# Moving four of six early weight loads behind two units' inputs, and one weight conversion behind a small product

## The chip, the core and the metric

The kernel runs on one core of a Trainium2 chip. The time is the device time of one execution in microseconds (us); less is better. Times of a run with the profiler on are given with their source. In the profile PE is the matrix engine (TensorE), PEld its weight loads, DVE VectorE, ACT ScalarE, POOL GpSimd, and SPq the queue of SyncE, which issues every DMA of this kernel.

## What is computed

Two blocks, one after the other, on float32 data:

```
# attention: batch 4, 8 heads, sequence 768, head size 48
f = 1 / (1 + exp(-f_logit))
for t in range(768):                       # per batch and head
    state = f[t][:, None] * state + outer(k[t], v[t])      # 48 x 48
    y[t]  = q[t] @ state
# mixer: x is y laid out as (4, 768, 384)
h  = (x^T @ U @ V)^T                        # U: 768 x 32, V: 32 x 768
u  = x + h
out = u + max(u @ w_ch1, 0) @ w_ch2         # w_ch1: 384 x 1536, w_ch2: 1536 x 384
```

The four mixer weights come in as 64-bit floats, all other inputs as 32-bit floats.

## The kernel before, in words

**Attention units.** The work of attention is cut into 16 units: a unit is one batch and two heads. A unit's inputs f, k, q and v are each loaded in two or three DMAs (`load`, L376; issued in L387 and L394, from unit 6 on also in L400). Rows of 48 floats make packets of 192 bytes, and a unit is 9 DMAs of 1,152 KB in all. f, k and q have two buffers each, v has three, so the loads of unit n wait until unit n-2 (for v: n-3) has been read. In the first stretch a unit runs through: transposes on PE (`pt`, L506), sigmoid on ACT (L527), two scans on DVE (L540, L558), products on DVE (L518), scores (`sc`, L589), the transposed keys (`kept`, L610), the states (`ds`, L626, scanned on DVE in L647), the output from the states (`y`, L664), then the output within chunks (`y`, L682), and a copy on ACT into the batch's `x` (L688). Ahead of the last matmuls of `y` stands a tiny copy on ACT (`seen`, L671).

**Mixer.** When the four units of a batch are done, its mixer starts: `low_rank` (`ph`, L146, copied by ACT in L149), `added_up` (`ph`, L154, copied by ACT in L156), `mix` (`pu`, L171, added to x by DVE in L161), `turn` (transposes `put`, L181, copied by ACT into `uT` in L182, for three pairs of row blocks), then the first large product `ch1` (`pz`, L193; relu on ACT in L200) and the second (L215 or L238). The mixer of a batch is woven into the attention of the next batch.

**Weights.** `weights` is a list of 27 tiles in this order: U, V in two pieces, 12 tiles of w_ch1 (called w1_0 to w1_11 here; 384 KB each as 64-bit words), 12 tiles of w_ch2. Each tile has a `start`, which issues its DMA (L55), and an `end`, which turns 64-bit floats into 32-bit floats: two instructions on ACT (L64, L65), three on DVE (L66 to L68), one on POOL (L69). U and V land in `w_raw` buffers, of which there are four. w1_0 to w1_5 ("staged": `FIRST = 6`) land in the three `zw` tiles, two in each, which the mixer needs only later. `ahead_by(n, loads)` (L76) starts the first n tiles at once and returns one call for each tile: call i starts tile i+n and then converts tile i.

**What sets the order.** PE, DVE and ACT run in the order in which the program is written (L748, L749). The DMAs stand in SyncE's queue in program order too, and the queue blocks on a DMA whose buffer is not free. In the loop over the first four units (L761 to L776) the order in the queue is: after unit 1's pieces, the v of unit 3 and then `ahead_by(early + FIRST, weights)`, so U, V, V and w1_0 to w1_5; after unit 2's pieces unit 4's f, k, q and v; after unit 3's pieces unit 5's. Behind the loop, L777 and L778 weave the conversions into the end of unit 3: U and the first V ahead of its last matmuls of `y`, and the second V, w1_0 and w1_1 behind its copy into `x`. These five calls also issue the loads of w1_6 to w1_10. Then the loop at L787 runs the mixer's pieces; from its third piece on (`i > 1`) each is followed by one more conversion. Piece 0 is `low_rank`, 1 `added_up`, 2 `mix`, 3 and 4 the first two `turn`, 5 the first `ch1`.

**Filler.** `busy(n)` (L754) issues matmuls on PE whose result nobody reads (`idle`, L756); the kernel has them at places where PE would stand still.

The last part of the kernel, `general_path`, runs only if the inputs are out of the range of the first path; with these inputs it does not run.

Of the kernel before, what the change touches and what calls it, by code (L numbers as in the profile page):

```python
# [20 lines left out]
RAW = 4  # L21
# [53 lines left out]

def ahead_by(n, loads):  # L76

    for start, _ in loads[:n]:
        start()

    def call(i):
        if i + n < len(loads):
            loads[i + n][0]()
        loads[i][1]()

    return [lambda i=i: call(i) for i in range(len(loads))]
# [237 lines left out]
def factored_path(ctx, tc, q, k, v, f_logit, moe_U, moe_V, moe_w_ch1, moe_w_ch2, out, ok):  # L324
# [11 lines left out]
    HP = H // 2  # L336
# [39 lines left out]
    def load(n, *names):  # L376

        b, hp = divmod(n, HP)
        for nm in names:
            if nm == "v":  # L380
                v_tiles[n] = three.tile([P, NBL, 2, D], F32, name="v_nat")
            for par in range(2):
                head = src[nm][b, 2 * hp + par]
                if nm == "v" and par:

                    for s in range(2):
                        nc.sync.dma_start(  # L387
                            out=v_tiles[n][(1 - s) * C : (2 - s) * C, :, par, :],
                            in_=head.rearrange("(c s p) d -> s p c d", s=2, p=C)[s],
                        )  # L390
                    continue
                if nm == "v" or n < TURNED:
                    dst = v_tiles[n] if nm == "v" else nat[n % 2][nm]
                    nc.sync.dma_start(out=dst[:, :, par, 0:D], in_=head.rearrange("(c p) d -> p c d", p=P))  # L394
                    continue
                head = head.rearrange("(c i) d -> i c d", i=NB)
                for part in range(2):
                    p0 = par * PAD + part * NB
                    n_ch = min(NB, D - part * NB)
                    nc.sync.dma_start(  # L400
                        out=raw[n % 2][nm][p0 : p0 + NB, :].rearrange("p (c d) -> p c d", d=NB)[:, :, 0:n_ch],
                        in_=head[:, :, part * NB : part * NB + n_ch],
                    )
# [51 lines left out]
    weights = [take_in(U, moe_U.rearrange("(c p) r -> p c r", p=P))]  # L455
    weights += [take_in(*pair) for pair in by_rows(V, moe_V, R)]
    early = len(weights)
# [10 lines left out]
    FIRST = 6  # L468
# [99 lines left out]
    def mixer(b):  # L568
        return Mixer(tc, b, x_tiles[b], U, V, w1, w2, sums if b else None, ident, blocks, out, two, three, zp, ps_big, ps_mm, b == 0)
# [128 lines left out]
    def front(n, *names):  # L698

        if n >= NU:  # L700
            return []
        if n not in ahead:
            ahead[n] = dict(zip(("gates", "keep", "keys", "read_back", "queries"), prepare(n)))
        return [ahead[n].pop(nm) for nm in names]

    def rear(n, *names):

        if not 0 <= n < NU:
            return []
        if n not in here:  # L710
            here[n] = dict(zip(("kept", "states", "scan", "scores", "read", "inner"), attend(n)))
        return [here[n].pop(nm) for nm in names if nm in here[n]]

    def steps(first, last):


        for n in range(first, last):
            yield from rear(n - 1, "scores") + rear(n, "kept") + front(n + 1, "gates", "keep", "keys")
            yield from rear(n - 1, "read")
            made = rear(n, "states", "scan")  # L720
            yield lambda: [f() for f in made]
            yield from front(n + 1, "read_back", "queries") + rear(n - 1, "inner")
            if n + 2 < NU:
                load(n + 2, "v")

    def attention(pieces, portions, todo):

        fill = Fill(todo, portions)
        for piece in pieces:
            fill()  # L730
            piece()
        fill.rest()

    def start_mixer(b, after):

        m = mixer(b)
        n = len(after) // 4
        pieces = after[:n] + m.before[:1] + after[n : 2 * n] + m.before[1:2] + after[2 * n : 3 * n]
        pieces += m.before[2:3] + after[3 * n :] + m.before[3:]
        for _, piece in pieces:  # L740
            piece()
        return m

    loads = weights

    ctx.enter_context(tc.manual_schedule(engines={nc.tensor.engine}))  # L748
    with tc.manual_schedule(engines={nc.vector.engine, nc.scalar.engine}):  # L749


        idle = ps_mm.tile([P, 512], F32, name="idle", tag="mm")

        def busy(n):  # L754
            for _ in range(n):
                nc.tensor.matmul(idle[:, 0:DM], lhsT=ident, rhs=ends[:, 0:DM], start=True, stop=True)  # L756

        busy(1)
        for piece in front(0, "gates"):
            piece()  # L760
        for n in range(HP):  # L761
            pieces = front(n, "keep", "keys") + rear(n - 1, "scan", "scores")
            pieces += [lambda: busy(3)] + rear(n, "kept") + front(n, "read_back", "queries")
            if n + 1 < HP:
                pieces += front(n + 1, "gates") + rear(n - 1, "read", "inner") + rear(n, "states")
            else:
                pieces += rear(n, "states") + rear(n - 1, "read") + rear(n, "scan", "scores") + rear(n - 1, "inner")
            for piece in pieces:
                piece()
            if n < 2:  # L770
                load(n + 2, "v")
            if n == 1:

                loads = ahead_by(early + FIRST, weights)
            elif n > 1:
                load(n + 2, "f", "k", "q", "v")  # L776
        for piece in rear(HP - 1, "read") + loads[:2] + rear(HP - 1, "inner") + loads[2 : early + 2]:  # L777
            piece()  # L778
        loads = loads[early + 2 :]

        m = mixer(0)
        start = m.before[:5] + m.firsts[0:1] + m.before[5:]
        idles = {1: 1, 2: 1}

        EARLY = 9
        second = chain(front(HP, "gates", "keep", "keys", "read_back", "queries"), steps(HP, 2 * HP + 1))
        for i, (_, piece) in enumerate(start + m.firsts[1:]):  # L787
            busy(idles.get(i, 0))
            piece()
            if loads and i > 1:  # L790
                loads.pop(0)()
            if i >= EARLY:
                next(second)()
        for f in loads:
            f()
        n = len(m.seconds) // (NBL // 2)
        todo, after = m.seconds[:-n], m.seconds[-n:]

        attention(second, 12 + 10 * HP - (len(start) + len(m.firsts) - 1 - EARLY), todo)
        m = start_mixer(1, after)  # L800
        for f in to_sum:
            f()
# [17 lines left out]
def general_path(ctx, tc, q, k, v, f_logit, moe_U, moe_V, moe_w_ch1, moe_w_ch2, out):  # L820
# [16 lines left out]
    HP = H // 2  # L837
# [70 lines left out]
    def load_unit(n):  # L908
        b, hp = divmod(n, HP)
        for nm in "fkq":  # L910
            for par in range(2):
                nc.sync.dma_start(
                    out=nat[n % NSLOT][nm][:, :, par, 0:D],
                    in_=src[nm][b, 2 * hp + par].rearrange("(c p) d -> p c d", p=C),
                )
        v_tiles[n] = three.tile([P, NCH, 2, D], F32, name="v_nat")
        for par in range(2):
            nc.sync.dma_start(
                out=v_tiles[n][:, :, par, :],
                in_=src["v"][b, 2 * hp + par].rearrange("(c p) d -> p c d", p=C),  # L920
            )

    load_weight = weight_loader(nc, two, nc.sync)
    weights = [load_weight(U, moe_U.rearrange("(c p) r -> p c r", p=P))]
# [148 lines left out]
    def mixer(b):  # L1073
        return Mixer(tc, b, x_tiles[b], U, V, w1, w2, None, ident, blocks, out, two, three, zp, ps_big, ps_mm)

    FILLS = NL + 3
    for n in range(NSLOT):
        load_unit(n)
    todo = [(1, f) for f in ahead_by(RAW - 1, weights)]
    for b in range(B):  # L1080
        fill = Fill(todo, HP * FILLS)
        for hp in range(HP):
            attention(b * HP + hp, fill)
        fill.rest()
        m = mixer(b)
        todo = m.before + m.main + m.after
# [59 lines left out]
```

## Time and profile before

| | |
|---|---|
| median of 5 runs | 502.48 us (499.28, 502.42, 502.48, 502.81, 504.44) |
| the profiled execution's own time | 502.67 us |
| its span from first to last instruction | 500.9 us (1.8 us lie around it) |
| PE busy, share of the span | 482.1 us, 96% |
| DVE busy, share | 279.3 us, 56% |
| ACT busy, share | 158.0 us, 32% |
| POOL busy, share | 36.4 us, 7% |
| DMA moved | 34.30 MB, of it 28.70 MB read |
| mean granted clock of TensorE | 0.987 |

The profile's page has the busy share of each engine in 40 slices of 12.5 us; a digit is tenths, 9 means 90% or more. The row PEclk is the TensorE clock that was granted, in tenths of full speed, and the row DMA the mean busy share of the 16 DMA engines. The chain of work that ended last goes back from the last instruction, at each step to what released it; "issue" in it is time for which the profile shows nothing that was waited for. The queue named "instruction" carries the fetches of the engines' own instructions.

### The profile page before, as it was taken

The numbers are of one execution on the slowest core, as the hardware profiler recorded it, in microseconds if no ns is written. First come the engines' busy times: TensorE is split into PE (matmuls) and PEld (weight loads), VectorE is DVE, ScalarE is ACT, GpSimd is POOL, SyncE is SP. The second block draws the span as 40 slices with busy tenths as digits, with TensorE's granted clock in tenths as the row PEclk, the third lists the DMA queues.
The fourth block names the chain that finished last, engine by engine and source line by source line (L and its number), as shares of the span: only waits on it lengthen the run. The fifth ranks groups of instructions, "written<-read, shape, count | busy, mean of one in ns | idle before, by whom it ended". The sixth has DMA issues, their size and how long they took to land.

```text
span 500.9 us, 11989 instructions
## 1 busy us (share of the span) xinstructions
PE 482.1 (96%) x5279; PEld 401.5 (80%) x5279; DVE 279.3 (56%) x402; ACT 158.0 (32%) x297; POOL 36.4 (7%) x49
## 2 busy tenths in 40 slices
PE   6896899999999999999999999999999999999995
PEld 4676588886666568898898788898899888999995
DVE  5884799788998667666764536632411431222232
ACT  3432675654444223324323222413311122101010
POOL 3000355442000000000000000000000000000000
PEclk9997899999999999999999999999999999999998
DMA  9989947675777423325434100100000000000001
GB/s 146 156 182 213 213 122 168 154 152 70 110 111 112 90 41 41 56 26 100 53 48 81 24 33 1 26 1 33 3 1 33 0 35 0 1 31 1 31 2 37
DMA packets 158676, 34.30 MB, mean 68 GB/s; under 512 B 149206, under 2 KB 157078, under 8 KB 158614
## 3 DMA queue, kind: packets, MB, share of 16 engines
q1 hardware_dynamic: 158614, 33.44, 36.4%
q8 instruction: 43, 0.70, 0.6%
q14 instruction: 19, 0.16, 0.1%
HBM read 28.70 MB, written 4.72 MB: 67 GB/s over the span
## 4 chain that ended last, share of the span: by engine, by line
PE 92%; DMA 2%; SPq 2%; DVE 1%; issue 1%; ACT 1%; DVEq 0%; ACTq 0%
PE pz L193 38%; PE pw L238 24%; PE po L215 10%; PE y L664 3%; PE y L682 3%; PE sc L589 3%; PE ds L626 2%; PE pt L506 2%; PE put L181 2%; PE pt L610 1%; SPq L394 1%; PE idle L756 1%; PE ph L146 1%; PE pu L171 1%; DMA f_raw<-in_f_logit_dram 1%
## 5 line engine op out<-in xcount | busy, mean ns | idle before, releaser
L193 PE MATMUL pz<-uT,w 128*128 128x256 f32 x864 | 196.0, 382 | 0.1
L193 PEld LDWEIGHTS pz<-uT,w 128*128 128x128 f32 x864 | 161.0, 190 | 22.4 <-issue 0.3
L200 ACT ACTIVATE z<-pz 128x512 f32<-128x512 f32 x63 | 37.6, 596 | 129.9 <-PE pz L193 125.8
L238 PE MATMUL pw<-w,z 128*128 128x192 f32 x324 | 56.5, 329 | 0.4 <-DVE o L161 0.4
L238 PE MATMUL pw<-zw,w_raw 128*128 128x192 f32 x324 | 55.9, 327 | 0.8 <-DVE o L161 0.8
L238 PEld LDWEIGHTS pw<-zw,w_raw 128*128 128x128 f32 x324 | 53.0, 190 | 2.2 <-DVE o L161 2.1
L238 PEld LDWEIGHTS pw<-w,z 128*128 128x128 f32 x324 | 52.8, 190 | 2.3 <-DVE o L161 1.6
L161 DVE TENSOR_TENSOR w_raw<-z 128x768 f32<-128x768 f32 x18 | 17.2, 955 | 56.3 <-ACT z L200 56.3
L540 DVE TENSOR_TENSOR_SCAN X<-fz,ends 128x768 f32<-128x768 f32 x16 | 28.1, 1757 | 10.3 <-ACT fz L535 5.1
L69 POOL TENSOR_TENSOR w<-w_y,w_r 128x384 int32<-128x384 int32 x24 | 30.2, 1259 | 36.0 <-DVE w_y L68 29.0
L558 DVE TENSOR_TENSOR_SCAN Y<-fz,starts 128x768 f32<-128x768 f32 x16 | 27.9, 1747 | 0.2
L596 DVE TENSOR_TENSOR A<-sc,causal 128x768 f32<-128x768 f32 x16 | 15.2, 949 | 20.4 <-PE sc L589 20.4
L215 PE MATMUL po<-w,zw 128*128 128x384 f32 x72 | 25.6, 499 | 0.0
L215 PE MATMUL po<-w,z 128*128 128x384 f32 x72 | 25.3, 496 | 0.0
L161 DVE TENSOR_TENSOR w_y<-x,pw 128x192 f32<-128x192 f32 x9 | 3.2, 354 | 38.2 <-ACT w_y L251 38.2
L652 ACT COPY st<-added 128x576 f32<-128x576 f32 x12 | 14.7, 1222 | 23.7 <-DVE added L647 23.7
L161 DVE TENSOR_TENSOR w_y<-w_y,pw 128x192 f32<-128x192 f32 x18 | 6.3, 349 | 25.5 <-PE pw L238 25.5
L215 PEld LDWEIGHTS po<-w,zw 128*128 128x128 f32 x72 | 12.9, 189 | 8.7 <-issue 1.2
L215 PEld LDWEIGHTS po<-w,z 128*128 128x128 f32 x72 | 13.1, 190 | 8.5 <-DVE o L161 0.6
L589 PE MATMUL sc<-qT,kz 48*64 48x64 f32 x768 | 15.9, 226 | 4.0 <-issue 4.0
L589 PEld LDWEIGHTS sc<-qT,kz 48*64 48x64 f32 x768 | 13.6, 138 | 7.7 <-issue 7.7
L238 PE MATMUL pw<-w,w_raw 128*128 128x192 f32 x108 | 19.2, 328 | 0.0
(101 smaller groups left out, 527.5 us busy)
## 6 DMA issues: line engine op xcount, KB each, us to landing
w_raw<-in_moe_w_ch_dram SPq DMA_DIRECT2D x18, 384.0 KB, 3.8
out_dram<-o SPq DMA_DIRECT2D x24, 192.0 KB, 2.0
v_nat<-in_v_dram SPq DMA_DIRECT2D x16, 144.0 KB, 3.0
v_nat<-in_v_dram SPq DMA_DIRECT2D x32, 72.0 KB, 2.8
zw<-in_moe_w_ch_dram SPq DMA_DIRECT2D x6, 384.0 KB, 6.1
f_raw<-in_f_logit_dram SPq DMA_DIRECT2D x20, 96.0 KB, 3.1
k_raw<-in_k_dram SPq DMA_DIRECT2D x20, 96.0 KB, 2.8
q_raw<-in_q_dram SPq DMA_DIRECT2D x20, 96.0 KB, 2.9
```

What stands on the lines that cost most here:

```text
L69: nc.gpsimd.tensor_tensor(dst.bitcast(I32), shaped(y.bitcast(I32)), shaped(r), ALU.add)
L161: nc.vector.tensor_tensor(*args)
L193: nc.tensor.matmul(pm[:, i * 2 * P : (i + 1) * 2 * P], lhsT=w1[:, m, o : o + P], rhs=uT[a][:, m, :], start=(m == 0), stop=(m == NDC - 1))
L200: nc.scalar.activation(z[a, c][:, k : k + 2, :].rearrange("p i t -> p (i t)"), pm, AF.Relu)
L215: nc.tensor.matmul(pm, lhsT=z[a, i // NI][:, i % NI, s * P : (s + 1) * P], rhs=w2[:, i, :], start=(i == 0), stop=(i == NFC - 1))
L238: nc.tensor.matmul(pm[:, n * HM : (n + 1) * HM], lhsT=lhs[:, i, :], rhs=rhs[:, i, :], start=(i == 0), stop=(i == NI - 1))
L540: nc.vector.tensor_tensor_scan(backwards(X, S - 1, S), backwards(f, S, S), backwards(ends, S - 1, S), 0.0, ALU.mult, ALU.add,)
L558: nc.vector.tensor_tensor_scan(Y, f[:, 0:S], starts, 0.0, ALU.mult, ALU.add)
L589: nc.tensor.matmul(sc[part[s ^ par], par, c * C : (c + 1) * C], lhsT=T["k"][rows[par], chunk[2 * c + s]], rhs=T["q"][rows[par], chunk[2 * ...
L596: nc.vector.tensor_tensor(T["A"], sc[:, :, 0 : NBL * C].rearrange("p h (c i) -> p h c i", i=C), causal.unsqueeze(1).unsqueeze(1).broadcast ...
L664: nc.tensor.matmul(o(c % 2, par, c // 2), lhsT=T["q"][rows[par], chunk[c]], rhs=T["st"][rows[par], c, :], start=(c <= 2), stop=False, skip ...
L682: nc.tensor.matmul(o(s, par, c), lhsT=T["A"][part[s ^ par], par, c, :], rhs=vt[part[s ^ par], c, par, :], start=False, stop=True, skip_gro ...
```

## The change

The six staged tiles are no longer started together. Five starts (U, V, V, w1_0, w1_1) stay where all nine stood, and the other four (w1_2 to w1_5) are issued behind the loads of units 4 and 5. `ahead_by` no longer starts anything at once. The conversion of w1_1 leaves its place behind unit 3's copy into `x`; it now follows `low_rank`, so it stands in ACT's and DVE's order between the copy of L149 and that of L156. Of the loads of w1_6 to w1_10, four are issued by the calls at the end of unit 3, and w1_10 goes with w1_1's call. In `general_path` the starts that `ahead_by` did are written out.

```diff
 def ahead_by(n, loads):
-    for start, _ in loads[:n]:
-        start()
     def call(i):
         if i + n < len(loads):
             loads[i + n][0]()
         loads[i][1]()
...
-    loads = weights
...
                 load(n + 2, "v")
             if n == 1:
-                loads = ahead_by(early + FIRST, weights)
+                for start, _ in weights[: early + 2]:
+                    start()
             elif n > 1:
                 load(n + 2, "f", "k", "q", "v")
-        for piece in rear(HP - 1, "read") + loads[:2] + rear(HP - 1, "inner") + loads[2 : early + 2]:
+        for start, _ in weights[early + 2 : early + FIRST]:
+            start()
+        loads = ahead_by(early + FIRST, weights)
+        for piece in rear(HP - 1, "read") + loads[:2] + rear(HP - 1, "inner") + loads[2 : early + 1]:
             piece()
-        loads = loads[early + 2 :]
+        loads = loads[early + 1 :]
...
             piece()
-            if loads and i > 1:
+            if loads and i != 1:
                 loads.pop(0)()
...
     todo = [(1, f) for f in ahead_by(RAW - 1, weights)]
+    for start, _ in weights[: RAW - 1]:
+        start()
```

## The prediction

> **What bounds the kernel now.** I read the page's slices first, to see where the matrix engine is not full.
>
> ```profile
> PE   6896899999999999999999999999999999999995
> ...
> PEclk9997899999999999999999999999999999999998
> DMA  9989947675777423325434100100000000000001
> ```
>
> From 62 us on PE stands at nine tenths or more, so time lost earlier is not made good later: what moves the first `pz` moves the end. The only weak place beyond the start-up is slices 3 and 4 (37 to 62 us), and the granted clock is down in the same slices. The busy times by stretch (columns: busy us and count of PE, PEld, DVE, ACT, POOL; then clock, DMA share, GB/s) narrow it.
>
> ```profile
> 36.00:40.00 4.00, 3.86 (x110) 2.87 (x111) 3.72 (x4) 1.99 (x3) 0.00 (x0) 1.00 1.03 313
> 40.00:44.00 4.00, 0.65 (x30) 0.51 (x23) 1.36 (x1) 0.28 (x2) 0.00 (x0) 0.99 1.19 273
> 44.00:48.00 4.00, 3.64 (x126) 3.50 (x125) 0.96 (x1) 0.64 (x1) 0.00 (x0) 0.50 0.94 162
> 48.00:52.00 4.00, 2.90 (x58) 2.10 (x58) 2.82 (x10) 2.90 (x10) 1.04 (x2) 0.50 0.70 135
> 52.00:56.00 4.00, 4.00 (x14) 1.48 (x8) 3.15 (x6) 2.26 (x6) 2.05 (x3) 0.73 0.93 160
> ```
>
> From 40 to 44 us PE does almost nothing, then its clock is halved. The chain of work that ended last says what PE waited for:
>
> ```profile
> 40.39 0.26 PE sc L589 x9
> 40.65 3.71 issue
> 44.36 1.20 PE sc L589 x28
> ...
> 50.20 0.65 ACT x L688
> ...
> 50.98 2.77 PE ph L146 x12
> ...
> 59.95 2.83 PE pz L193 x12
> ```
>
> "issue": no semaphore. PE stops in the middle of `sc`, whose operands are all there. Counting PE's recorded instructions, it stops after number 1473; a smaller stop of the same kind (0.33 us at 25.07) is after 705. The difference is 768, three times 256, and the page has 43 instruction packets for 10,636 PE instructions, about one per 247. So PE ran out of instructions. The last view is the DMA traffic in two windows, 36 to 41.5 us and 40 to 42 us (packets, MB, share):
>
> ```profile
> q1 hardware_dynamic: 1857, 1.79, 104.9%
> ```
> ```profile
> q1 hardware_dynamic: 949, 0.69, 110.1%
> q8 instruction: 1, 0.02, 3.5%
> ```
>
> PE began on its last block in hand at 35.78 us; the packet that brings the next one starts at 41.82 and takes 1.13, and PE resumes 1.41 later. Before it the engines move nearly only 1 KB packets (115 of 1,857 are under 512 B), the staged tiles; it comes when they are through. That was a 6.04 us wait. Where only unit loads were queued, the same wait (new block entered to packet started) was 2.19, 1.02, 2.59, 0.88, 1.42 and 2.08 us.
>
> **The change, part by part.**
>
> *Four tiles leave the queue ahead of this fetch.* At 35.78 us w1_0's packets are about through and w1_1 is under way. A tile takes about 1.2 us (landings of the staged tiles: 37.68, 38.78, 39.89, 41.29, 42.44, 44.18), so w1_1 is through at about 37.2. SyncE then issues unit 4: two or three DMAs of 144 KB are out before the fetch is asked for, at 0.9 us each (unit 0's land at 3.71, 4.49, 5.49, 6.40). The fetch starts at 37.2 if only w1_1 is ahead, at 39.9 if three unit DMAs are too. In the old kernel everything issued until then went first, so I take two, 39.0. PE resumes at 39.0 + 1.13 + 1.41 = 41.5: a gap of 0.9 (0 to 1.8) in place of 3.7.
>
> [...]
>
> *The next block.* From there PE needs 256 instructions: the rest of `sc` 0.66, `y` 0.92, `y` 1.24 and the wait for `seen` 0.5 (full-clock rows of units 1 and 2), 3.3 us, to 44.8. The next block needs 2.0 (unit loads queued; 0.9 to 2.6) + 1.2 + 1.41 = 4.6, to 46.1: a new gap of 1.3 (0.2 to 2). Then `y` 0.92 and the copy into x 0.7: x is ready at 47.8 (46.5 to 48.9), against 50.85.
>
> *The clock.* In the old trace it is halved at 43.94, for 10.24 us. [...] If it fell all the same, `y` would take its 1.85 instead of 0.92 and `ph` its 2.77 instead of about 1.4, some 2.4 us in all.
>
> *The moved conversion.* w1_1's has 0.55 + 0.55 us on ACT, 0.35 + 1.04 + 0.56 on DVE, 1.0 on POOL. In its old place at full clock it would hold up the copy of L149 by about a microsecond, which the slow clock hid (`ph` ended at 53.75, the copy began at 53.79). Behind x now stand the second V 0.62 and w1_0 1.1 with a 0.28 wait for POOL, x + 2.0; copy 0.5; w1_1 1.1; copy 0.5: x + 4.1. Its DVE part is done at about x + 5.0, just ahead of the additions to x (`pu` needs 1.0 from the copy). POOL has w1_1 ready at x + 6.1. Then add 1.0, transposes 0.9, copy 0.8: the first `pz` at x + 8.0 = 55.8. The old trace needed 59.95 - 50.85 = 9.1.
>
> *The four tiles, later.* They stand behind 18 DMAs. From the last staged tile's landing (44.18) to the end of unit 5's (about 58.8: the next DMA, issued at 55.89, lands at 59.73) the old kernel took 14.6 us for these 18. From w1_1's landing now: 38.78 + 14.6 = 53.4, and w1_2 lands at 54.4 (53.3 to 55.5), w1_3 to w1_5 1.1 apart. Nothing waits for w1_3 to w1_5. But w1_2's two ACT instructions stand ahead of `uT`'s copy in ACT's order, and its wait for the DMA holds that copy: 54.4 + 1.1 + 0.8 + 0.2 = 56.5 for the first `pz`. This is later than 55.8, so w1_2's landing sets the new start; x may come up to 0.7 later at no cost. Behind w1_2's wait on DVE and POOL stand only its own steps and the next tiles'; w1_2 and w1_3 are first used 8.7 us after the first `pz` (68.6 against 59.95), so 65, and are converted by about 60. w1_6 to w1_9 follow in SyncE's queue, landing about 59 to 63 in place of 59.73 to 64.78: no cost. Units 4 and 5 land earlier; nothing waited for them. The starts written out in the path that does not run cost nothing.
>
> *Sum.* First `pz` at 56.5 instead of 59.95: 3.4 us less; from there PE is full. The profiled execution took 502.67 (span 500.9 and 1.8 around it), 0.19 over the median: 502.48 - 3.4 = 499.0.
>
> **The rivals.**
>
> *Part of the gain (20 in 100).* Either the fetch waits behind all of unit 4's DMAs (gap 1.8 or more) and the clock falls again, or w1_2 lands 1 to 3 us later than worked out. For: unit loads had waits up to 2.6 too. [...] 499.9 to 502.4; with the clock down x comes at about 50, `pz` at 58.8, time 501.3.
>
> *The fetch doesn't come sooner (8).* [...] The gap and the half clock stay, the time is 502.5. Against: the packet follows the last 1 KB packets.
>
> *Slower (9): the late tile stops ACT and with it PE.* PE has done its transposes at about x + 7.9. If w1_2 lands after 57.9, `pz` starts later than before (57.9 + 2.1 = 60). [...] For: unit loads move at only 150 GB/s and 2.3 MB of them are ahead. Against: it needs 3 us more than the old trace took for the same DMAs.
>
> *As worked out (63).* 498.0 to 499.9: gain 2.6 to 4.5, from the bounds of w1_2's landing (53.3 to 55.5) and of x.
>
> **How the numbers follow.** A measurement here can tell about 0.5%, 2.5 us. Faster by more than that: all of the main case and 1 of 20 of the second, 0.64. Slower: 0.09. Within: 0.27. The prediction is the main case, 499.0. The range, 497.8 to 502.6, takes in the main case and those that leave the gap or part of it; it leaves out the slower one and some 5 in 100 below.
>
> **What would show it.** Right: the instruction packet of 41.8 starts at about 39, the "issue" in `sc` is under 2 us, the clock is 1.00 from 44 to 54, x is copied at 47 to 49, ACT waits for the DMA of w1_2 at 53 to 55, the first `pz` is at 56 to 57. Wrong: a stop of over 3 us in `sc`; a half clock anywhere before 70; w1_2 landing after 57; waits on PE after 60 that the old trace doesn't have.

## The result, and the profile after

The changed kernel takes 500.28 us (median of 27 runs, 498.79 to 502.32); the kernel before, over its 48 runs on the same chips, 502.35. The ratio is 0.9961, 95% interval 0.9951 to 0.9972: 0.4% faster, 2.1 us. The prediction was 499.0 (497.8 to 502.6). The direction was right and the time is in the range. The gain is 2.1 in place of 3.4 us. That is less than the 0.5% for which the prediction gave 64 in 100, and the time lies in its second case (499.9 to 502.4), not in the main one. The profiled execution took 500.1 us against 502.67 before, span 498.3 against 500.9.

The slices of the page, PE, clock and DMA:

```profile
PE   7996999999999999999999999999999999999995
...
PEclk9999999999999999999999999999999999999998
DMA  9979956684777323406234100100000000000001
```

The weak digit has moved from the fourth to fifth slice of PE to the fourth alone, and the clock row no longer shows the dip. The same stretches as before (PE, PEld, DVE, ACT, POOL busy; clock, DMA share, GB/s):

```profile
36.00:40.00 4.00, 3.79 (x95) 2.64 (x98) 3.69 (x4) 1.68 (x3) 0.00 (x0) 1.00 1.07 225
40.00:44.00 4.00, 3.18 (x170) 3.04 (x160) 2.32 (x2) 1.23 (x3) 0.00 (x0) 1.00 0.99 169
44.00:48.00 4.00, 1.35 (x56) 0.97 (x48) 1.97 (x6) 1.71 (x7) 1.04 (x2) 1.00 1.04 163
48.00:52.00 4.00, 3.82 (x15) 1.41 (x16) 2.10 (x7) 2.36 (x8) 1.44 (x2) 0.57 1.07 180
```

From 40 to 44 us PE is at work, 170 matmuls against 30. The hole is now in the next row, 44 to 48 us, and the clock falls after it, to 0.57 in one row, instead of after 44 and for three rows. The chain of work that ended last:

```profile
40.69 0.26 PE sc L587 x9
40.95 0.82 issue
41.77 0.73 PE sc L587 x31
...
44.45 0.25 PE y L680
44.70 1.73 issue
46.43 0.95 PE y L680 x47
47.38 0.02 issue
47.40 0.65 ACT x L686
48.05 0.14 issue
48.18 2.78 PE ph L144 x12
...
57.24 2.83 PE pz L191 x12
```

The stop in `sc` is 0.82 us in place of 3.71. Counted in PE's instructions it is at the same place, after number 1473. The second stop, 1.73 us, comes after 1729, one block of 256 on. x is there at 48.05 (50.85 before), the first `pz` starts at 57.24 (59.95 before). From there to the end it is 441.06 us, before 440.99: PE is full from there, and the 2.7 us stay as they are to within 0.1.

In the trace the instruction packet that PE waits for in `sc` starts at 38.84 us, 2.48 after PE entered its last block at 36.37. In the DMA traffic from 37 to 38.8 us there is no instruction packet, from 38.8 to 40.4 us there is one:

```profile
q1 hardware_dynamic: 1509, 0.51, 123.4%
```
```profile
q1 hardware_dynamic: 1047, 0.20, 88.1%
q8 instruction: 1, 0.02, 5.7%
```

### The profile page after: what moved, and what is told of

Its sections match the earlier page's. It is cut to its first block, busy times and chain, and to the rows that moved or that the text cites. A ratio compares the mean times of both kernels' runs of the same rounds, so it can differ in the third digit from the quotient of the medians.

```text
span 498.3 us, 11989 instructions
## 1 busy us (share of the span) xinstructions
PE 482.4 (97%) x5279; PEld 400.7 (80%) x5279; DVE 278.5 (56%) x402; ACT 157.9 (32%) x297; POOL 36.4 (7%) x49
## 4 chain that ended last, share of the span: by engine, by line
PE 93%; DMA 2%; DVE 1%; issue 1%; ACT 1%; SPq 0%; DVEq 0%; ACTq 0%
PE pz L191 39%; PE pw L236 24%; PE po L213 10%; PE y L662 3%; PE y L680 3%; PE ds L624 3%; PE sc L587 3%; PE pt L504 2%; PE idle L752 2%; PE put L179 2%; PE pt L608 2%; PE ph L144 1%; PE pu L169 1%; DMA f_raw<-in_f_logit_dram 1%; DMA k_raw<-in_k_dram 1%
## 5 line engine op out<-in xcount | busy, mean ns | idle before, releaser
L236 PE MATMUL pw<-w,z 128*128 128x192 f32 x324 | 56.5, 329 | 0.4 <-DVE o L159 0.4
L680 PEld LDWEIGHTS y<-v_nat,A 64*64 64x64 f32 x768 | 12.9, 134 | 7.7 <-issue 6.3
L236 PEld LDWEIGHTS pw<-w,w_raw 128*128 128x128 f32 x108 | 17.7, 190 | 1.1 <-issue 1.1
```

Source lines behind the costliest of these rows:

```text
L236: nc.tensor.matmul(pm[:, n * HM : (n + 1) * HM], lhsT=lhs[:, i, :], rhs=rhs[:, i, :], start=(i == 0), stop=(i == NI - 1))
L680: nc.tensor.matmul(o(s, par, c), lhsT=T["A"][part[s ^ par], par, c, :], rhs=vt[part[s ^ par], c, par, :], start=False, stop=True, skip_gro ...
```

## The experiments

Ratios are to the kernel before on the same chip, with their 95% interval. "The wait" is, as in the prediction, the time from PE's entry into its last block of instructions to the start of the packet that brings the next one; a block is 256 instructions, counted from the stops at 1473 and 1729.

**Each part alone.** The changed kernel with w1_1's conversion back in its old place:

```diff
-... + loads[2 : early + 1]:
+... + loads[2 : early + 2]:
-        loads = loads[early + 1 :]
+        loads = loads[early + 2 :]
-            if loads and i != 1:
+            if loads and i > 1:
```

> The changed kernel, but the conversion of w1_1 back in its old place ahead of low_rank. Theory (the gain is the shorter instruction wait from the moved loads; ph runs at half clock, so ACT has time for w1_1 before the copy of h): about as the changed kernel, 500.3 us, gap in sc about 0.8, copy of h at most 0.3 later. Rival (the moved conversion carries the gain): 501.5 us or more, the copy of h about 1 us later after the end of ph than in the changed kernel.

0.9963 (0.9946 to 0.9979), the same as the changed kernel's 0.9961. In its profile the stop in `sc` was 1.81 us, where 0.8 was expected: the wait was 3.69 us, though the same DMAs stood ahead as in the changed kernel (2.48). The clock was halved for 10.24 us from 42.11, `ph` took 2.77 us, and the copy of h began 0.04 us after the end of `ph`.

The kernel before with only the conversion moved (the same three lines the other way):

> The kernel before, with only the conversion of w1_1 moved behind low_rank; all six staged tiles load together as before. Theory: the stop of 3.7 us in sc and the half clock of about 10 us stay, time 502.3 us within 0.5. Rival (the moved conversion carries the gain): 501.3 us or less.

0.9990 (0.9978 to 1.0002). Its profile has a wait of 5.27 us, a stop of 2.90 us in `sc` and the half clock for 10.24 us. So the moved loads carry the gain; of the moved conversion nothing could be measured in either direction. In both profiles `ph` ran at half clock, under which the conversion is hidden; at full clock the old place was not profiled.

**How many tiles stand ahead of the instruction packet.** The changed kernel with four tiles in the early place:

```diff
-                for start, _ in weights[: early + 2]:
+                for start, _ in weights[: early + 4]:
-        for start, _ in weights[early + 2 : early + FIRST]:
+        for start, _ in weights[early + 4 : early + FIRST]:
```

> The changed kernel with four staged tiles (w1_0 to w1_3) in the early place instead of two; w1_4 and w1_5 stay behind. Theory (the instruction packet queues behind whatever DMAs were issued before it was asked for, a tile costs 1.2 us, a unit DMA 0.9 us): the packet starts at 39.8 to 41 us (38.84 with two tiles, 41.82 with six), the stop in sc is 1.7 to 2.9 us, time 500.5 to 501.8. [...]

0.9980 (0.9966 to 0.9995). The packet started at 40.51, as expected from the queue, and 5.06 us after the block was entered. It took 1.43 us rather than 1.13, and PE stopped for 3.18 us, a little more than expected. The clock was then halved for 13.65 us.

```profile
43.41 1.22 PE L587 MATMUL sc<-qT,kz 48*64 48x64 f32 x34 [3.18 <-issue]
```

A stop of 0.8, as with two tiles, is out.

**Nothing ahead of it.** The changed kernel, with all DMAs behind w1_1 held until unit 3's masked scores exist, by a copy of two columns on POOL into each buffer (of the edit, the main lines):

```diff
+        late = units[HP - 1]["A"]
+        held = [place() for _ in range(2, FIRST)]
+        for raw_k in held:
+            nc.gpsimd.tensor_copy(raw_k.bitcast(F32)[:, 0:2], late[:, :, 0, 0])
...
+        for n in range(HP, HP + 2):
+            for nm in "fkq":
+                nc.gpsimd.tensor_copy(nat[n % 2][nm][:, 0, :, 0], late[:, :, 0, 0])
+            load(n, "f", "k", "q", "v")
```

> The changed kernel, but w1_2 to w1_5, w1_6 and units 4 and 5 are all held until the masked scores A of unit 3 are there (a tiny POOL copy from A into each buffer ahead of its DMA), with w1_2 to w1_5 first and units 4 and 5 behind them. So nothing but w1_0 and w1_1 is in the DMA queue between about 37 and 42.5 us. Theory (the queue ahead of the instruction packets makes both stops): the packet for the block that runs dry in sc starts at about 37.3, no stop there over 0.3 us; the second stop at most 0.5; no half clock between 44 and 54; x copied at about 45.5, first pz at 53.5 to 54.5, time 496.5 to 498. Rival (the fetch has a fixed latency, or the stop has another cause): stops of 0.8 and 1.7 as in the changed kernel, 500 to 500.5, or slower where the late unit loads are missed.

The stops went as expected, the time did not: 1.0036 (1.0021 to 1.0051). The packet for the stop in `sc` started at 38.10 (37.3 expected), and `sc` ran through in one piece (a step of 0.1 us at the block's end). The next packet started 1.14 us after it was due (2.02 in the changed kernel), the second stop was 0.46 us, and the first `pz` began at 54.50. The clock was halved all the same, for 3.41 us from 45.26, and `ph` took 2.77 us; full clock was expected. Then ACT waited, in the view of waits from 55 to 75 us (engine and line, what it waited for, us, times, longest):

```profile
ACT w_y L64 <- DMA w_raw<-in_moe_w_ch_dram: 5.4, 1, 5.4
PEld pz L191 <- issue: 4.5, 1, 4.5
PE pz L191 <- ACT z L198: 4.1, 1, 4.1
```

The row names w1_6, which now stood behind units 4 and 5 in SyncE's queue and landed at 65.74. Behind ACT's wait in its order stood the relu for which PE waited 4.1 us, and within this wait the clock fell, for 6.83 us from 65.74. This is what the prediction has on the slower side, a late tile that stops ACT and with it PE, with another tile.

**The same with the weight tiles first.** As the last one, but units 4 and 5 are held until unit 3's x is there and stand behind w1_9:

```diff
+        late = x_tiles[0][:, 0, 6 * D : 6 * D + 2]
+        for n in range(HP, HP + 2):
+            for nm in "fkq":
+                nc.gpsimd.tensor_copy(nat[n % 2][nm][:, 0, :, 0], late)
+            load(n, "f", "k", "q", "v")
```

> As the run with the DMAs held, but the loads of units 4 and 5 are held until unit 3's part of x is there and stand behind w1_6 to w1_9 as well, so that no weight tile waits behind unit loads. Theory: the stops stay under 0.5 us, first pz at about 54.5 as with the DMAs held, and the 5.4 us wait of ACT for w1_6 that ate the gain there is gone: 497 to 498.5 us, faster than the changed kernel by some 2.5. Rival (early unit loads are needed, or the weights are late anyway): a wait of over 3 us behind the first pz, 500 or more.

498.40 us (7 runs), ratio 0.9948 (0.9919 to 0.9978). Profile, PE in order of time:

```profile
40.14 0.97 PE L598 MATMUL sc<-qT,kz 48*64 48x64 f32 x45
...
44.02 0.91 PE L691 MATMUL y<-v_nat,A 64*64 64x48 f32 x47 [0.65 <-issue]
45.78 1.48 PE L144 MATMUL ph<-x,U 128*32 128x384 f32 x12 [0.84 <-ACT x L697]
...
53.45 2.83 PE L191 MATMUL pz<-uT,w 128*128 128x256 f32 x12
```

`sc` in one piece, `ph` at full clock in 1.48 us, the first `pz` 3.8 us earlier than in the changed kernel. Of that 1.6 are given back: from `pz` to the end it takes 442.6 us, with a 1.2 us wait of PE at 74. The chain there goes from a later weight tile (w1_10, landed at 70.67) through its conversion on ACT and DVE and a scan on DVE to the relu for which PE waits. With the filler of the next run added to it, to see whether the two together keep `ph` at full clock:

> The run with the tiles first and the filler ahead of low_rank, together. If both theories hold: ph at full clock and short stops, first pz at 53 to 54, 496 to 497.5 us. If the filler doesn't hold the clock: as the run with the tiles first, or 0.5 slower.

498.33 us, 0.9935 (0.9917 to 0.9954): the lowest median of the study, though above the 496 to 497.5 expected. It beats the kernel before; its interval still touches the changed kernel's (0.9951 to 0.9972) and contains the ratio without the filler, so the filler is not shown to do anything here.

**Can filler hold the clock?**

```diff
-        idles = {1: 1, 2: 1}
+        idles = {0: 2, 1: 1, 2: 1}
```

> The changed kernel with two filler products (busy(2)) on PE ahead of low_rank, where PE waits 0.8 us for the copy into x. [...] Rival (the clock is set by the stop alone, filler can't hold it): no change or 0.5 slower, 500.3 to 500.8.

0.9963 (0.9951 to 0.9975), no change, although in its profiled execution `ph` ran at full clock (498.95 us). One execution does not say which clock is usual, so both kernels were profiled twice more:

> The changed kernel once more, for a second look at its clock. If the half clock in ph is its usual state: ph takes 2.8 us and the time is 500 or more. If it was an accident of that one execution: ph 1.5 us, about 498.8. In both, stops of 0.5 to 1.8 us in sc and of 0.5 to 1.8 at the block after it.

> The changed kernel a third time, for the same question: ph 2.8 us with 500 or more, or ph 1.5 us with about 498.8.

> The changed kernel with two filler products ahead of low_rank, a second look. If the filler holds the clock: ph 1.5 us again, 499. If its full clock was an accident of when the clock windows fell: ph may be 2.8 us, 500 to 501.

> The changed kernel with the filler a third time, for the same question: ph 1.5 us and 499 if the filler holds the clock, ph 2.8 us in some looks and 500 to 501 if it does not.

| execution | stops, us | half clock, us | `ph`, us | first `pz` | time |
|---|---|---|---|---|---|
| changed | 0.82, 1.73 | 48.14 to 51.55 | 2.78 | 57.24 | 500.10 |
| changed, second | 0.71, 1.45 | none | 1.48 | 55.24 | 498.47 |
| changed, third | 0.55, 1.75 | 48.79 to 52.20 | 2.59 | 57.66 | 500.32 |
| filler | 0.70, 1.45 | none | 1.49 | 55.63 | 498.95 |
| filler, second | 0.11, 1.55 | 45.85 to 49.27 | 1.49 | 56.98 | 499.93 |
| filler, third | 0.98, 1.45 | 47.11 to 50.52 | 2.28 | 57.13 | 500.17 |

(In the third execution of the changed kernel the first stop was at the end of the block before, after number 1217, in filler matmuls, and PE did not stop in `sc`.) The filler does not decide it.

Three executions do not tell how often the clock falls, but every execution on record has the mean granted clock of its span. The two in the table without a fall have 0.999 and 0.998, the four with one have 0.994 to 0.996. Of the 29 executions of the changed kernel that stand with the result, the first of the table among them, one has 0.999 and all others 0.996 or less; 13 have 0.992 or less, below each of the four with a single fall. So the fall is the usual case in the changed kernel. With the filler 4 of 22 have 0.998 or more, too few to tell from 1 of 29. With the weight tiles first it is 4 of 7, with tiles first and filler 7 of 11: the share is larger where the second stop is shorter (0.65 and 0.63 us).

What decides it is open. The steps of the clock's record in these traces lie whole multiples of 3.41 us apart (10.59 to 48.14 us in the changed kernel is eleven, 51.55 to 495.29 is 130); a window is here one such stretch of 3.41 us, placed by these steps. In the four windows ahead of the falls of the table PE was busy for 0.91 to 1.70 us, in the two windows around the second stop that no fall followed for 1.87 and 2.05. Busy time alone does not sort them: with four tiles first a window with 1.98 us was followed by a fall, with the DMAs held one with 2.18. These two had matmuls of 48 and 64 columns only, and the two that kept the clock had half of their time in products of 128 x 384. That the place of the windows against the second stop, and the kind of matmul in them, decide is my reading, and not shown by an experiment. The row of the second execution of the changed kernel, 48 to 52 us, beside the 0.57 above:

```profile
48.00:52.00 4.00, 3.98 (x26) 1.79 (x20) 3.59 (x9) 2.84 (x7) 1.45 (x2) 1.00 1.20 171
```

**Does the stop go with the instruction count?** The kernel before with 16 tiny products, 64 PE instructions, more in unit 0:

```diff
             for piece in pieces:
                 piece()
+                if n == 0 and piece is pieces[2]:
+                    for _ in range(16):
+                        nc.tensor.matmul(idle[0:8, 0:8], lhsT=ident[:, 0:8], rhs=ends[:, 0:8], start=True, stop=True)
```

> The kernel before, with 16 tiny products more on PE in the first unit (64 PE instructions, in time in which PE stands still). Loads as before. Theory (PE stops where a block of 256 instructions ends whose successor is not there): the place moves by exactly 64 instructions; sc runs through at 40 us, and the stop is in the output from the states (y, L664 of the kernel before) some 128 PE instructions behind the old place or more, 1.5 to 3 us long; time 500.5 to 502.3. Rival (the DMA traffic itself holds PE up at 40 to 44 us): the stop stays in sc at 40.6 us with 3.7 us.

```profile
40.51 0.87 PE L664 MATMUL y<-st,qT 48*64 48x48 f32 x26
42.83 0.63 PE L664 MATMUL y<-st,qT 48*64 48x48 f32 x17 [1.44 <-issue]
```

The stop has left `sc`: PE stops after instruction 1473 of the new count, which is 64 instructions earlier in the work, in the `y` ahead of `sc`. The expectation named a later `y`; this one is where the count of 256 puts it. A hold by the traffic itself, in `sc`, is out. The time was no better, 1.0018 (1.0000 to 1.0037): in its profile the clock also fell at 22.54 us and twice more.

## Why the prediction was right or wrong

**The fetch waits behind the staged tiles: right.** Packet at 38.84 (39.0 forecast), stop of 0.82 (0.9). Shown by the counts. With six tiles out the wait is 6.04, 5.27 and 4.88 us (the kernel before, with the conversion moved, with the 64 instructions more), with four 5.06, with two 2.48 to 3.69 in six executions (1.97 in the third of the table, where PE entered this block 1.4 us later), and with nothing behind w1_1 1.99 to 2.66 in three. So two tiles and more than two are clearly apart, six and four are not, and the unit DMAs ahead cost about 1 us at most. With two tiles the stop at this place was 0.11 to 1.81 us in the six; why it varies was not tried.

**The next block: right in kind, 0.4 short.** Stop of 1.73 against 1.3. The fetch took what was forecast (2.02 + 1.07 + 1.57 against 4.6), but PE was through with the block after 2.93 us (41.77 to 44.70), not 3.3. With the DMAs held the stop is 0.46 to 0.65, so most of it too is queueing behind the unit loads.

**The clock: the step that failed.** The sum has full clock after short stops in it: `ph` 1.4. No run shows that short stops are enough for it: in two of three profiles of the changed kernel (stops of 0.82 and 1.73, 0.55 and 1.75 us) the clock was halved for 3.41 us, and `ph` took 2.78 and 2.59; in the third (0.71 and 1.45) it stayed full, and `ph` took 1.48. By the mean clock of all executions the fall is the usual case. The execution without it has the first `pz` at 55.24 and the time 498.47, and the two with it 500.10 and 500.32, so a fall costs 1.6 to 1.9 us where the prediction had put it at 2.4. This is more than the 1.3 us between 499.0 and the median; the tile below gave part of it back. In these runs the clock fell after a window with 0.13 us of PE work (the kernel before), and also after one with 2.18 us (the DMAs held). The prediction had named "a half clock anywhere before 70" as a sign of being wrong, and it came. The half clock was cut from 10.24 to 3.41 us in the first profile, so part of this gain came all the same; the rest was lost after the second stop.

**The moved conversion: no cost, no gain,** as far as 0.3% can be told. The copy of h began at once after `ph` in both places, at half clock. In the execution at full clock the chain of work runs through the moved steps, as the prediction had them, just ahead of the additions to x:

```profile
50.28 1.17 DVE w_y L66
...
51.87 0.56 DVE w_y L68
52.43 0.91 DVE x L159
```

The `pu` that the first addition needs was there at about the same time, so this costs 0.1 us at most.

**The late tile: landed earlier than worked out, and did not bind at half clock.** w1_2 landed at 53.21 (54.4 forecast): in SyncE's queue of the trace the two loads of w1_2 and w1_3 (issued from 48.29) stand ahead of unit 5's v (50.37), though the program has them behind it. So the queue does not keep wholly to program order; the description of the kernel above, which says that it does, is wrong in this. ACT came to w1_2 at 53.30, just after it had landed, and did not wait. The chain from x to the first `pz` was 9.2 us at half clock (8.0 forecast at full clock, 7.6 in the second execution). So in the first execution x and not w1_2 set the first `pz`. In the second, at full clock, w1_2 landed at 53.24 and ACT did wait for it, 2.04 us. With this landing the prediction's own sum, landing + 1.1 + 0.8 + 0.2, gives 55.3, and the first `pz` began at 55.24. There the two paths end together: the path by w1_2 was right, and its landing was forecast 1.2 us too late.

**So the time is near in part by luck.** The first `pz` was forecast for 56.5 and came at 57.24. At full clock, as forecast, it came at 55.24. Two errors lie on opposite sides and offset each other in part: the clock was taken as full, and the tile's landing as too late.

**From `pz` on: right.** 441.06 against 440.99.

**What stays open.** The traces don't say what keeps the clock; PE's busy time in a window alone does not sort them. And why a packet at times starts sooner than the DMAs issued before it (in the early units waits of 0.75 and 0.80 us in the changed kernel, 0.88 and 1.02 in the kernel before) was not tried.

## What to carry to other kernels

An "issue" stop on PE inside a group whose operands are all there is worth counting. The stops here lie multiples of 256 instructions apart (after 705, 1473 and 1729), and PE resumed 1.2 to 1.6 us after the end of an instruction packet: it was out of instructions. What helped was to have fewer bytes in the DMA queues a few us earlier, when PE entered its last block: from there the packet started after 2.48 us in place of 6.04, and the stop was 0.82 us in place of 3.71. The large loads that nobody needed yet stood just ahead of a dense stretch of small matmuls, where 256 instructions lasted only 2.9 us (41.77 to 44.70 in the changed kernel). They could go behind, but then every later tile in the queue has to be followed: the kernel that emptied the queue first lost all of the gain (1.0036) to one weight tile behind the unit loads, for which ACT waited 5.4 us.

## What the runs showed that was not expected

- TensorE's clock was halved after windows in which PE was busy for 0.91 us (changed kernel) and 2.18 us (DMAs held) of 3.41 us, the latter in small matmuls only; it stayed down for 3.41, 6.83, 10.24 or 13.65 us, multiples of 3.41.
- The same kernel has executions with and without the fall, 498.5 and 500.1 to 500.3 us in the three profiles. A single profile may show either; the mean clock of the other executions says which is usual.
- After its stops PE resumed 1.2 to 1.6 us after the instruction packet's end: 1.41 in the kernel before, 1.26 in the second execution of the changed kernel, 1.57 after the second stop of its first.
